# Early raw-key scores for half a token tile, cosines split by parity, joins put first: one core of a Trainium2 chip

## The chip, the cores and the metric

The kernel runs on one core of a Trainium2 chip. The core has a matrix engine (TensorE, PE in the rows; PEld is its load of the stationary operand), a vector engine (VectorE, DVE), an activation engine (ScalarE, ACT), a general engine (GpSimd, POOL) and a sync engine (SyncE, SP), whose queue issues nearly all transfers between device memory and the on-chip memory. Each engine works through its own instructions in the order in which they were written, and waits for others by semaphores. The metric is the time of one execution on the device, in microseconds.

## The reference

Three stages follow each other: attention that keeps the 32 best scores of each row, a gated feed-forward layer, and a second layer with a cosine.

```python
# q, k, v: (4, 8, 576, 64); the result of each stage is (2304, 512)
scores = scale * np.matmul(q, k.transpose(0, 1, 3, 2))
kth = np.partition(scores, -top_k, axis=-1)[..., -top_k:-top_k + 1]   # top_k = 32
scores = np.where(scores >= kth, scores, -1000000000.0)
scores = scores - np.max(scores, axis=-1, keepdims=True)
attn = np.exp(scores); attn = attn / (np.sum(attn, axis=-1, keepdims=True) + 1e-09)
x = np.matmul(attn, v)                       # laid out as (2304, 512)
g = x @ w_gate                               # (512, 1536)
x = (g * (1.0 / (1.0 + np.exp(-g))) * (x @ w_val)) @ w_out
h = x @ w_in                                 # (512, 2048)
out = (h * np.cos(h)) @ w_out2               # (2048, 512)
```

## The kernel before

The 2304 tokens are 18 tiles of 128 rows. A batch has 576 rows, four and a half tiles, so the fifth tile (number 4, rows 512 to 639) holds the last 64 rows of batch 0 and the first 64 of batch 1; tile 13 is cut in the same way. Tiles are grouped into ten chunks: two of one tile, then eight of two.

**Order of work.** The order of every engine's instructions is made when the program is built. Each piece of work is a Python generator that yields steps: an engine, a cost, a function that emits the instructions, and a due time. A planner (class `Plan`) keeps a clock for each engine and always emits, of the steps that are ready by its clock, the one with the smallest due time. What it emits is fixed: on the chip each engine takes its instructions in that order. So a change of a due time, a cost or a wait in the generators moves instructions on all engines.

**Attention.** A unit is one tile of one head: 144 units, `unit_proc`. Its scores are made on PE (lines 590 and 597) in one bank pair `sc`, ACT copies them to a tile `s` (line 602; five such tiles), DVE finds the 32 largest by four MAX8 and three MATCH_REPLACE8 (lines 627 and 630), POOL makes two bounds, ACT masks and exponentiates (lines 658 and 669), PE transposes (line 691) and multiplies with V (lines 744 and 747). In the first three chunks (tiles 0 to 3, all of batch 0) the scores are fp32 matmuls on raw keys `kr` that four early loads bring in. From the fourth chunk on, keys and queries are split into two parts of the rounded format (high part by ACT, line 496, and rest by POOL, line 500), and a score takes two matmuls for each half of the 576 keys. So the 64 rows of batch 0 in tile 4 need split keys of batch 0: eight tiles, two loads each (line 489).

**First feed-forward layer.** `turned_gemm_proc` (line 992) and `gemm_proc` (line 902) multiply x with the gate and value weights into the banks `gv`, and `wout_proc` (line 1066) multiplies the product with the output weights `wo` into the banks `y`. The wo weights are converted once (ACT, and POOL on line 248), stored, and loaded again for each chunk into two buffers (lines 375 and 377), each load after PE is through with the buffer.

**Second layer.** The first product is made with seven products in place of eight (a Strassen scheme): 32 pairs of rows of h, `h_proc`, PE line 1401. Each pair uses three banks. ACT copies partial sums aside (lines 1432 and 1488) and DVE joins them (lines 1445, 1466, 1473, 1479); PE goes on in a bank after the join on 1466 (c22) or the copy on 1479. The weights of the seven products come in four groups, added on DVE (line 1268) and split (ACT line 1284, DVE line 1287). The rows of h are stored to device memory, some with the cosine already applied (lines 1535 to 1552), some raw. Before the change rows whose block f of 128 columns lies in the second or fourth group of four are raw, and take the cosine late, after they are loaded again. The last stage loads h in pieces of four blocks (line 1627), splits them (lines 1643 and 1647) and multiplies (line 1672).

## Time and profile before

| | us |
|---|---|
| median of 3 runs (1238.5 to 1436.85) | 1239.03 |
| the profiled execution | 1239.47 |
| its span, first to last instruction | 1237.7 |

A profile row names an engine, a line of the kernel, an operation, and tiles as out<-in. Busy is the time in which an engine has an instruction at work; a matrix engine that is busy is not always at its best, since matmuls overlap. A wait is put down to the instruction that released it last. The granted clock of the matrix engine is 1.00 at its higher level, 2.4 GHz, and 0.50 at 1.2 GHz.

### The profile page before, as it was taken

To read this page: it belongs to the slowest core of one execution; us is meant where nothing else is said; L and a number is where in the kernel's file an instruction comes from. 1 tells how busy PE (TensorE), PEld (TensorE's weight loads), DVE (VectorE), ACT (ScalarE), POOL (GpSimd) and SP (SyncE) were. 2 spreads that over 40 slices of the span, in tenths; PEclk is the share of its full clock that TensorE was granted. 3 is DMA by queue.
4 is the path that set the end of the run, shared out by engine and by line. 5 is a ranking of instruction groups with operands and counts; after the bars stand their busy time and mean duration, and the time that the engine had idled before them with its cause. 6 is when DMAs were issued, how large, how long until landed. Compare 5 with 4: busy or idle time off the path is not lost.

```text
span 1237.7 us, 23277 instructions
## 1 busy us (share of the span) xinstructions
PE 1179.8 (95%) x7720; PEld 1021.3 (83%) x7720; DVE 1003.4 (81%) x1984; ACT 936.6 (76%) x2085; POOL 575.6 (47%) x1036
## 2 busy tenths in 40 slices
PE   6699988999999999999999999998999999999998
PEld 3477646898888898888898898988899998888887
DVE  6999999999999999998999996267867778544441
ACT  4789988899889889897898887445757668765651
POOL 4898976777677776776777765300000000000000
PEclk9899989999999999999999999999999999999999
DMA  7555555665555565566555533463344376433430
GB/s 256 165 176 163 178 173 186 205 203 178 185 171 170 189 196 154 169 185 187 188 166 174 162 105 95 154 212 117 134 139 135 130 228 212 144 107 115 124 106 26
DMA packets 138984, 199.95 MB, mean 162 GB/s; under 512 B 19312, under 2 KB 88432, under 8 KB 138864
## 3 DMA queue, kind: packets, MB, share of 16 engines
q1 hardware_dynamic: 138704, 198.40, 50.6%
q8 instruction: 61, 1.00, 0.3%
q14 instruction: 59, 0.48, 0.1%
q10 hardware_dynamic: 160, 0.07, 0.0%
HBM read 152.28 MB, written 46.14 MB: 160 GB/s over the span
## 4 chain that ended last, share of the span: by engine, by line
PE 56%; DMA 7%; ACT 7%; DVE 4%; POOL 4%; issue 2%; SPq 0%; POOLq 0%; ACTq 0%; DVEq 0%
PE b L1672 16%; PE b L1401 13%; PE gv L902 10%; PE y L1066 7%; PE av L747 3%; PE sc L597 2%; PE gvl L902 2%; PE tp L691 2%; DMA kx<-in_kT 2%; DVE m L627 1%; DVE w L630 1%; DMA w2d<-w_raw 1%; DMA wo<-wo 1%; DMA qx<-in_qT 1%; DMA w_raw<-in_w 1%
## 5 line engine op out<-in xcount | busy, mean ns | idle before, releaser
L627 DVE MAX8 m<-w 128x8 f32<-128x576 f32 x432 | 310.9, 747 | 1.8
L902 PE MATMUL gv<-x,w 128*128 128x256 f32 x2016 | 284.0, 288 | 2.2 <-ACT hg L869 2.1
L902 PEld LDWEIGHTS gv<-x,w 128*128 128x128 f32 x2016 | 259.2, 190 | 9.3 <-ACT hg L869 3.5
L630 DVE MATCH_REPLACE8 w<-m,w 128x576 f32<-128x576 f32 x288 | 213.2, 742 | 0.0
L1672 PE MATMUL b<-w2o,gp 128*128 128x512 f32 x864 | 202.1, 395 | 0.0
L1672 PEld LDWEIGHTS b<-w2o,gp 128*128 128x128 f32 x864 | 162.1, 188 | 39.0
L1401 PE MATMUL b<-xc,w 128*128 128x288 f32 x1344 | 184.2, 298 | 6.1 <-DVE h L1466 5.6
L1401 PEld LDWEIGHTS b<-xc,w 128*128 128x128 f32 x1344 | 181.5, 189 | 7.6 <-DVE h L1466 6.3
L1066 PE MATMUL y<-wo,gh 128*128 128x512 f32 x400 | 148.7, 414 | 5.2 <-DMA wo<-wo 2.5
L627 DVE MAX8 m<-s 128x8 f32<-128x576 f32 x144 | 107.6, 747 | 17.6 <-ACT s L602 15.9
L658 ACT ACTIVATE e<-s,b 128x576 f32<-128x576 f32 x144 | 114.2, 794 | 9.2 <-POOL b L641 9.0
L669 ACT ACTIVATE e<-e,b 128x576 f32<-128x576 f32 x144 | 114.2, 793 | 2.8 <-POOL b L645 0.2
L602 ACT ACTIVATE s<-sc 128x576 f32<-128x576 f32 x144 | 95.4, 663 | 21.4 <-PE sc L590 15.8
L630 DVE MATCH_REPLACE8 w<-m,s 128x576 f32<-128x576 f32 x144 | 106.8, 742 | 0.0
L691 PE MATMUL tp<-ident,e 128*128 128x128 f32 x648 | 98.9, 276 | 6.4 <-ACT pt L697 3.1
L697 ACT ACTIVATE pt<-tp 128x512 f32<-128x512 f32 (+1 forms) x216 | 101.5, 501 | 4.3 <-PE tp L691 2.9
L1066 PEld LDWEIGHTS y<-wo,gh 128*128 128x128 f32 x400 | 74.7, 188 | 28.0 <-issue 4.1
L597 PE MATMUL sc<-K,q 128*128 128x288 f32 (+1 forms) x512 | 92.2, 307 | 2.6 <-ACT s L602 2.3
L691 PEld LDWEIGHTS tp<-ident,e 128*128 128x128 f32 x648 | 77.9, 142 | 16.9 <-ACT pt L697 6.7
L1066 PE MATMUL y<-wo,gl 128*128 128x512 f32 x208 | 85.6, 418 | 6.1 <-POOL gl L965 3.0
L965 POOL TENSOR_TENSOR gl<-vv,gh 128x256 fp32r<-128x256 f32 x84 | 62.0, 738 | 42.5 <-ACT gh L961 29.0
L597 PEld LDWEIGHTS sc<-K,q 128*128 128x128 f32 (+1 forms) x512 | 73.4, 184 | 8.3 <-ACT s L602 3.7
(115 smaller groups left out, 2093.7 us busy)
## 6 DMA issues: line engine op xcount, KB each, us to landing
wo<-wo SPq DMA_DIRECT2D x96, 512.0 KB, 3.7
gr<-gd SPq DMA_DIRECT2D x72, 256.0 KB, 3.1
w_raw<-in_w SPq DMA_DIRECT2D x32, 511.8 KB, 4.3
V<-in_vP SPq DMA_DIRECT2D x52, 256.0 KB, 3.0
w<-in_w SPq DMA_DIRECT2D x24, 511.5 KB, 5.6
kx<-in_kT SPq DMA_DIRECT2D x64, 144.0 KB, 3.2
wo<-wo SPq DMA_DIRECT2D x36, 256.0 KB, 3.0
gd<-r SPq DMA_DIRECT2D x32, 288.0 KB, 2.2
```

The costliest lines, as they stand in the source:

```text
L597: nc.tensor.matmul(sc[:r1, s, :HALF], q[:, a, (t - t0) * 128:(t - t0) * 128 + r1], k[:, s * HALF:s * HALF + HALF], start=a == 0, stop=a == 1)
L602: nc.scalar.activation(st["s"], sc[:, :, :HALF], AF.Copy)
L627: nc.vector.max(out=st["m"][:, 8 * i:8 * i + 8], in_=st["w"] if i else st["s"])
L630: nc.vector.match_replace(out=st["w"], in_to_replace=st["m"][:, 8 * i:8 * i + 8], in_values=st["w"] if i else st["s"], imm_value=LOWEST)
L658: nc.scalar.activation(st["e"], st["s"], AF.Prelu, bias=st["b"][:, 1:2], scale=SCALE, alpha=STEEP)
L669: nc.scalar.activation(st["e"], st["e"], AF.Exp, bias=st["b"][:, 2:3], scale=1.0, accum_out=smT[c, p, g][:, j:j + 1])
L691: nc.tensor.transpose(st["ps"][:, j - j0], e[:, j * 128:j * 128 + 128], ident)
L697: nc.scalar.activation(pt[:, j0:j1], st["ps"][:, :j1 - j0], AF.Copy)
L902: nc.tensor.matmul(gv[g], W1[f, kk // 2][:, a, g, kk % 2], m, start=kk == 0 and i == 0, stop=kk == KT - 1 and i == 2)
L1066: nc.tensor.matmul(bank, m, w, start=f == 0 and n == 0, stop=f == NF1 - 1 and n == len(terms) - 1)
L1401: nc.tensor.matmul(ps[b], w[:, a, side, kk], x[:, e, kk], start=start and kk == 0 and m == 0, stop=kk == 1 and m == 2, skip_group_check=True)
L1672: nc.tensor.matmul(st["o"], g[:, a, cs], W2O[f][:, b], start=f == 0 and i == 0, stop=f == NF2 - 1 and i == 2)
```

## The change

Eight units' upper 64 rows, those of batch 0 in tile 4, no longer get their scores from split keys. At the start, 64 columns of q for each head (`qe`, with the other head's half of the contraction cleared) are multiplied with the raw keys as fp32, into the banks of the first layer, which are not in use yet; ACT copies the scores to `se`, and four stores bring them to a new tensor `sd` in device memory. The units of tile 4 then compute all 128 rows with batch 1's keys, ACT copies only the lower 64 rows to `s`, and a load on SP's queue brings the upper 64 from `sd`. The first product of the first layer waits until all early scores are copied (`ev_edged`). Split keys of batch 0 are no longer made.

In the second layer, raw rows of h are now those with odd f, not those of the second and fourth group, and the pieces and the order of the last stage's products follow (`members`). The joins and ACT's copies before them are due 90 us before the pair's time, not 30 (all such lines alike, two of them shown). The banks of the pairs rotate over eight from the sixth pair on (`BOTH`), not from the seventh.

```diff
@@ -42,7 +42,7 @@
-BOTH = 6
+BOTH = 5
@@ -56,6 +56,7 @@
+EDGE_DUE = 40.0
@@ -404,7 +405,7 @@
 
     kb_first, kb_last = {}, {}
     for (c, p, h, b), u in kfirst.items():
-        if c < RAWC:
+        if c < RAWC or b == 0:
             continue
         kb_first.setdefault((b, p, h), u)
         kb_last[b, p, h] = max(kb_last.get((b, p, h), 0), klast[c, p, h, b])
@@ -419,8 +420,6 @@
     r_kp = Ring(1)
 
     def k_due(b, p, h):
-        if not b:
-            return due_unit(kb_first[0, 0, 0]) - 60.0 + 2.0 * (2 * p + h)
         return due_unit(kb_first[b, p, h]) - 26.0
 
     def q_due(c, p, g):
@@ -438,7 +437,77 @@
         return i if c < RAWC else RAWC * NP + (i - RAWC * NP) * 2 + h
 
     def k_index(b, p, h):
-        return 1 + NP + kvis[b, p, h]
+        return 2 + 2 * NP + kvis[b, p, h]
+
+    EDGE = S % 128
+    TE = S // 128
+    sd = dram.tile([NP, 128, S], F32, name="sd")
+    r_edge = [Ring(1) for _ in range(2)]
+    ev_edge = [Event() for _ in range(NP)]
+    ev_edged = Event(2 * NP)
+    edge = {}
+
+    def edge_proc():
+
+        def clear():
+            edge["q"] = att.tile([128, NP, 2, EDGE], F32, tag="K", name="qe", bufs=r_k.n)
+            nc.vector.memset(edge["q"], 0.0)
+
+        yield "DVE", 0.5, clear, -1.0, True
+
+        def load():
+            for h in range(2):
+                rows = slice(64 * h, 64 * h + 64)
+                nc.sync.dma_start(edge["q"][rows, :, h],
+                                  qT[:, rows, TE * 128:TE * 128 + EDGE].rearrange("p d n -> d p n"))
+
+        t = yield "DMA", 1.0, load, 2.0, True
+        for p in range(NP):
+            for h in range(2):
+                plan.start(edge_score(p, h), t)
+
+    def edge_score(p, h):
+        n = 2 * p + h
+        due = EDGE_DUE + n
+        yield ev_kr[p]
+        yield r_edge[h].gate(p)
+        ps = gvt if h == 0 else yt
+
+        def qk():
+            for s in range(2):
+                nc.tensor.matmul(ps[s][64 * h:64 * h + EDGE, :HALF], edge["q"][:, p, h],
+                                 KR[p][:, s * HALF:s * HALF + HALF])
+
+        t = yield "PE", 1.25, qk, due, True
+        if n == 2 * NP - 1:
+            r_k.free(1 + NP, t, plan)
+
+        def copy(s):
+            if (p, "s") not in edge:
+                edge[p, "s"] = att.tile([128, S], F32, tag="K", name="se", bufs=r_k.n)
+            rows = slice(64 * h, 64 * h + EDGE)
+            nc.scalar.activation(edge[p, "s"][rows, s * HALF:s * HALF + HALF], ps[s][rows, :HALF], AF.Copy)
+
+        if n and not h:
+            yield ev_edge[p - 1]
+        yield "ACT", 0.33, lambda: copy(0), due, True
+        t = yield "ACT", 0.33, lambda: copy(1), due, False
+        if not h:
+            ev_edge[p].set(t, plan)
+        r_edge[h].free(p, t, plan)
+        if not h:
+            edge[p, "n"] = Event(2)
+            plan.start(edge_store(p, due))
+        edge[p, "n"].set(t, plan)
+        ev_edged.set(t, plan)
+
+    def edge_store(p, due):
+        yield edge[p, "n"]
+        t = yield "DMA", 1.1, lambda: nc.sync.dma_start(sd[p], edge[p, "s"]), due + 2.0, True
+        r_k.free(2 + NP + p, t, plan)
+        ev_sd[p].set(t, plan)
+
+    ev_sd = [Event() for _ in range(NP)]
 
     def k_raw_proc(p):
 
@@ -579,9 +648,11 @@
             yield ev_qr[c, p]
         else:
             for b, r0, r1 in segs:
-                yield ev_k[b, p, h]
+                yield ev_k[b, p, h] if b else ev_sd[p]
             yield ev_q[c, p, g, h]
             q = Q[c, p, g, h]
+        split_row = c >= RAWC and segs[0][0] == 0
+        cuts = [x for x in segs if x[0]]
         yield r_s.gate(u)
 
         def qk():
@@ -591,6 +662,8 @@
                                      KR[p][:, s * HALF:s * HALF + HALF])
                 return
             for b, r0, r1 in segs[::-1]:
+                if not b:
+                    continue
                 k = K[b, p, h]
                 for s in range(2):
                     for a in range(2):
@@ -599,19 +672,25 @@
 
         def copy():
             st["s"] = att.tile([128, 2, HALF], F32, tag="s", name="s", bufs=r_s.n)
-            nc.scalar.activation(st["s"], sc[:, :, :HALF], AF.Copy)
+            if split_row:
+                nc.scalar.activation(st["s"][EDGE:], sc[EDGE:, :, :HALF], AF.Copy)
+                nc.sync.dma_start(st["s"][:EDGE].rearrange("p a b -> p (a b)"), sd[p, 64 * h:64 * h + EDGE])
+            else:
+                nc.scalar.activation(st["s"], sc[:, :, :HALF], AF.Copy)
 
         yield r_sc.gate(u)
-        end = yield "PE", 0.575 * len(segs) if c >= RAWC else 0.98, qk, due - SC_LEAD, True
+        end = yield "PE", 0.575 * len(cuts) if c >= RAWC else 0.98, qk, due - SC_LEAD, True
         if h and (c, t) == (RAWC - 1, SIZES[c] - 1):
             r_k.free(1 + p, end, plan)
         for b, r0, r1 in segs:
-            if c >= RAWC and kb_last[b, p, h] == u:
+            if c >= RAWC and b and kb_last[b, p, h] == u:
                 r_k.free(k_index(b, p, h), end, plan)
         if t == t0 + n - 1 and (h or c >= RAWC):
             r_q.free(q_index(c, p, g, h), end, plan)
         end = yield "ACT", 0.53, copy, due - SC_LEAD + 1.0, True
         r_sc.free(u, end, plan)
+        if split_row:
+            yield "-", 2.5, lambda: None, due, True
         st["s"] = st["s"].rearrange("p a b -> p (a b)")
         yield r_w.gate(u)
         yield r_m.gate(u)
@@ -984,6 +1063,7 @@
             yield ev_gemm[c, 2 * fp - 1]
         yield ev_x[c]
         ring, i = r_gv[fp % 2], GV0[c] + fp // 2
+        yield ev_edged
         yield ring.gate(i)
         bank = gvt[fp % 2].rearrange("p (f g n) -> p f g n", f=2, g=2)
 
@@ -1431,7 +1511,7 @@
                 snaps[name] = pb().tile([128, HN], F32, tag=f"s{name}", name="s", bufs=ring.n)
                 nc.scalar.activation(snaps[name], ps[b], AF.Copy)
 
-            t = yield "ACT", 0.33, fn, due + offset - 30, True
+            t = yield "ACT", 0.33, fn, due + offset - 90, True
             return t
 
         def row(r):
...
@@ -1519,7 +1599,10 @@
     r_s1, r_s2, r_s3 = Ring(2), Ring(1), Ring(1)
     ev_wfree = {(q, n): Event() for q in range(NF2 // 4) for n in range(SEVEN)}
 
-    early = [n for n in range(NCB * NF2) if n % NF2 // 4 not in LATE]
+    def group_of(f):
+        return f // 8 * 2 + f % 2
+
+    early = [n for n in range(NCB * NF2) if group_of(n % NF2) not in LATE]
     turn_of = {n: i for i, n in enumerate(early)}
 
     def cosine(i, h, width, due):
@@ -1611,6 +1694,9 @@
         (t, m) for t in range(AHEAD, NTOK // 128) for m in range(NG)]
     place = {x: n for n, x in enumerate(ORDER)}
 
+    def members(m):
+        return slice(m // 2 * 8 + m % 2, m // 2 * 8 + 8, 2)
+
     def piece_proc(t, m):
         n = place[t, m]
         due = o_due(n) - 6.0
@@ -1625,7 +1711,7 @@
             st["x"] = pools["pb"].tile([128, 2, HN], F32, tag="xr", name="gr", bufs=r_xr.n).rearrange(
                 "p a b -> p (a b)")[:, :DM]
             nc.sync.dma_start(st["x"].rearrange("p (f n) -> p f n", f=4),
-                              gd[:, 4 * m:4 * m + 4, t * 128:t * 128 + 128])
+                              gd[:, members(m), t * 128:t * 128 + 128])
 
         end = yield "DMA", 1.2, load, due - 6.0, True
         ev_gt[n].set(end - 2.0, plan)
@@ -1658,21 +1744,21 @@
         for m in range(NG):
             n = place[t, m]
             yield ev_gp[n]
-            for f in range(4 * m, 4 * m + 4):
+            for v, f in enumerate(range(NF2)[members(m)]):
                 yield ev_w2o[f]
                 if f == 0:
                     yield ring.gate(index)
 
-                def part(f=f, n=n):
+                def part(f=f, n=n, v=v):
                     if f == 0:
                         st["o"] = bank_tile(number)
                     g = GP[n]
-                    cs = slice(f % 4 * 128, f % 4 * 128 + 128)
+                    cs = slice(v * 128, v * 128 + 128)
                     for i, (a, b) in enumerate(((0, 0), (1, 0), (0, 1))):
                         nc.tensor.matmul(st["o"], g[:, a, cs], W2O[f][:, b], start=f == 0 and i == 0,
                                          stop=f == NF2 - 1 and i == 2)
 
-                end = yield "PE", 0.7, part, o_due(n) + f % 4 * 0.7, False
+                end = yield "PE", 0.7, part, o_due(n) + v * 0.7, False
             r_xc.free(SEVEN * NCB + n, end, plan)
         yield r_ot.gate(t)
 
@@ -1687,6 +1773,7 @@
 
     for p in range(NP):
         plan.start(k_raw_proc(p))
+    plan.start(edge_proc())
     for c, p in ev_qr:
         plan.start(q_raw_proc(c, p))
     for i, (_, kind, *which) in enumerate(split):
```

The order on three engines moves as follows. On PE, at the start of the program (`kr` raw keys, `qr` and `qe` queries, `sc` scores, `tp` transposes, `rx` normalising factors); before:

```order
L590 MATMUL sc<-kr,qr 128x288 x14
L691 MATMUL tp<-ident,e 128x128 x9
L794 MATMUL tp<-ident,rx 128x128
L590 MATMUL sc<-kr,qr 128x288 x2
L744 MATMUL av<-pt,vtail_106 128x128
L747 MATMUL av<-pt,V 64x128 x8
L590 MATMUL sc<-kr,qr 128x288 x2
L691 MATMUL tp<-ident,e 128x128 x9
```

and after the change:

```order
L661 MATMUL sc<-kr,qr 128x288 x12
L478 MATMUL gv_100<-kr,qe 64x288
L478 MATMUL gv_101<-kr,qe 64x288
L478 MATMUL y_102<-kr,qe 64x288
L478 MATMUL y_103<-kr,qe 64x288
L661 MATMUL sc<-kr,qr 128x288 x2
L770 MATMUL tp<-ident,e 128x128 x8
L478 MATMUL gv_100<-kr,qe 64x288
L478 MATMUL gv_101<-kr,qe 64x288
L770 MATMUL tp<-ident,e 128x128
L478 MATMUL y_102<-kr,qe 64x288
L478 MATMUL y_103<-kr,qe 64x288
L873 MATMUL tp<-ident,rx 128x128
```

The early scores stand between the sixth and the tenth unit's scores; the rest keeps its place.

On SP's queue, where the fourth chunk's scores begin (`wo` the two weight buffers, `wo_65` their store, `kx` and `qx` keys and queries to be split, `y` results of the first layer); before:

```order
L514 DMA qx<-in_qT 64x2x256 x2
L1111 DMA y_63<-yo 128x2x128
L375 DMA wo<-wo_65 128x512 x3
L1111 DMA y_63<-yo 128x2x128
L489 DMA kx<-in_kT 64x576 x2
L375 DMA wo<-wo_65 128x512 x3
L489 DMA kx<-in_kT 64x576 x2
L541 DMA V<-in_vP 128x512
```

and after:

```order
L558 DMA kx<-in_kT 64x576 x2
L1191 DMA y_63<-yo 128x2x128
L376 DMA wo<-wo_65 128x512 x2
L677 DMA s<-sd 64x576
L1191 DMA y_63<-yo 128x2x128
L376 DMA wo<-wo_65 128x512 x2
L677 DMA s<-sd 64x576
L583 DMA qx<-in_qT 64x2x256 x2
```

The key loads of batch 0 are gone, and the loads of the early scores stand behind weight loads, two before each of the first two.

On DVE, in the second layer, around the third group of weights (`w_14` to `w_20` split weights, `wr` their sums, `h` joins, `r` cosines); before:

```order
L1287 TENSOR_TENSOR w_14_11544<-wr,w_14_11544 128x512
L1287 TENSOR_TENSOR w_15_11555<-wr,w_15_11555 128x512
L1268 TENSOR_TENSOR wr<-wr 128x512
L1287 TENSOR_TENSOR w_19_11566<-wr,w_19_11566 128x512
L1268 TENSOR_TENSOR wr<-wr 128x512
L1287 TENSOR_TENSOR w_16_11589<-wr,w_16_11589 128x512
L1268 TENSOR_TENSOR wr<-wr 128x512
L1287 TENSOR_TENSOR w_17_11603<-wr,w_17_11603 128x512
L1287 TENSOR_TENSOR w_20_11576<-wr,w_20_11576 128x512
L1287 TENSOR_TENSOR w_18_11609<-wr,w_18_11609 128x512
L1466 TENSOR_TENSOR h<-b,s_11521 128x288
L1473 TENSOR_TENSOR h<-b,s 128x288
```

and after, where line 1348 is 1268 of before, 1367 is 1287, 1525 is 1445, 1546 is 1466, 1553 is 1473 and 1559 is 1479:

```order
L1553 TENSOR_TENSOR h<-b,s 128x288
L1367 TENSOR_TENSOR w_14_11518<-wr,w_14_11518 128x512
L1546 TENSOR_TENSOR h<-b,s_11491 128x288
L1367 TENSOR_TENSOR w_15_11530<-wr,w_15_11530 128x512
L1348 TENSOR_TENSOR wr<-wr 128x512
L1525 TENSOR_TENSOR h<-b,s 128x288
L1348 TENSOR_TENSOR wr<-wr 128x512
L1559 COPY h<-b 128x288
L1367 TENSOR_TENSOR w_16_11567<-wr,w_16_11567 128x512
L1367 TENSOR_TENSOR w_17_11579<-wr,w_17_11579 128x512
L1348 TENSOR_TENSOR wr<-wr 128x512
L1367 TENSOR_TENSOR w_19_11533<-wr,w_19_11533 128x512
```

The joins stood behind the seven splits and stand between them now.

## Rows read from the trace of the kernel before

**Rows 1.** Page, part 1: busy time, share of the span, instructions.

```profile
PE 1179.8 (95%) x7720; PEld 1021.3 (83%) x7720; DVE 1003.4 (81%) x1984; ACT 936.6 (76%) x2085; POOL 575.6 (47%) x1036
```

**Rows 2.** Busy time by stretch, us from the span's start.

```profile
core 0: us, PE busy (x) PEld busy (x) DVE busy (x) ACT busy (x) POOL busy (x), PEclk, DMA share, GB/s
...
27.00:64.00 37.00, 23.90 (x146) 16.82 (x145) 35.78 (x79) 29.52 (x64) 31.41 (x60) 0.91 0.54 175
...
128.00:230.00 102.00, 90.36 (x509) 64.38 (x508) 97.25 (x197) 93.14 (x213) 78.22 (x118) 0.97 0.57 179
230.00:757.00 527.00, 517.47 (x3896) 462.49 (x3894) 509.25 (x1050) 457.30 (x1116) 376.48 (x702) 1.00 0.55 173
757.00:850.00 93.00, 91.32 (x644) 83.24 (x644) 46.03 (x93) 44.99 (x107) 19.59 (x34) 1.00 0.51 162
850.00:890.00 40.00, 33.85 (x230) 32.14 (x229) 30.61 (x55) 29.55 (x60) 0.00 (x0) 0.96 0.33 114
890.00:1030.00 140.00, 140.00 (x1052) 140.00 (x1051) 104.04 (x193) 94.36 (x184) 0.00 (x0) 1.00 0.47 161
1030.00:1238.00 208.00, 204.10 (x883) 164.46 (x881) 99.78 (x152) 119.52 (x202) 0.00 (x0) 1.00 0.39 115
```

**Rows 3.** Waits of PE, 128 to 230: total us, times, longest.

```profile
PE y L1066 <- POOL wo L248: 3.2, 3, 2.7
PE y L1066 <- DMA wo<-wo: 2.7, 1, 2.7
PE sc L597 <- ACT s L602: 2.3, 4, 0.8
```

**Rows 4.** The same table by stretch, at three stretches of lower clock.

```profile
157.80:161.20 3.40, 3.40 (x17) 1.72 (x16) 3.37 (x8) 2.61 (x5) 3.32 (x4) 0.50 0.35 98
171.50:174.90 3.40, 3.40 (x12) 2.29 (x11) 3.29 (x9) 2.04 (x5) 2.23 (x4) 0.50 0.52 162
861.00:864.40 3.40, 3.40 (x15) 3.39 (x15) 1.91 (x5) 2.21 (x5) 0.00 (x0) 0.50 0.33 107
```

**Rows 5.** Timeline of PE, early: start, us, what, count [idle before <- releaser].

```profile
30.49 1.14 PE L590 MATMUL sc<-kr,qr 128*128 128x288 f32 x4
...
51.93 0.43 PE L794 MATMUL tp<-ident,rx 128*128 128x128 f32 x1 [4.04 <-POOL rx L783]
...
64.29 1.03 PE L992 MATMUL gv<-w,xw 128*128 128x256 f32 x4
```

**Rows 6.** Chain that ended last, second layer; timeline of PE, tile 4's first score.

```profile
886.63 144.27 PE b L1401 x1080
...
172.19 2.87 PE L597 MATMUL sc<-K,q 128*128 128x288 f32 x8
```

**Rows 7.** Tile kx, 90 to 250: ns min/median/max; POOL's timeline, first and eighth.

```profile
L496 ACT ACTIVATE K<-kx x16: 669/690/747, 99.9 to 241.5; 128x576 fp32r<-128x576 f32 x16
L500 POOL TENSOR_TENSOR K<-kx,K x16: 1399/1410/1699, 101.8 to 243.1; 64x576 fp32r<-64x576 f32 x16
...
DMA to landing us min/median/max: 2.6/2.9/3.8
...
151.69 1.40 POOL L500 TENSOR_TENSOR K<-kx,K 64x576 fp32r<-64x576 f32 x1
```

**Rows 8.** Waits of DVE, 128 to 230.

```profile
DVE m L627 <- ACT s L602: 1.4, 4, 0.6
```

**Rows 9.** Waits of SP's queue, 165 to 250.

```profile
SPq L375 <- PE y L1066: 4.9, 4, 2.1
```

**Rows 10.** Waits of PE, 850 to 890; timelines of DVE and PE there.

```profile
PE b L1401 <- DVE h L1466: 5.6, 3, 3.2
PE b L1401 <- DVE h L1479: 0.6, 1, 0.6
...
858.68 1.89 DVE L1287 TENSOR_TENSOR w<-wr,w 128x512 fp32r<-128x512 f32 x3
860.48 0.45 DVE L1466 TENSOR_TENSOR h<-b,s 128x288 f32<-128x288 f32 x1
...
860.99 3.25 PE L1401 MATMUL b<-xc,w 128*128 128x288 f32 x12 [3.20 <-DVE h L1466]
885.02 1.05 PE L1401 MATMUL b<-xc,w 128*128 128x288 f32 x6 [1.02 <-DVE h L1466]
```

**Rows 11.** Page, part 5 (busy, mean ns | idle before); part 6's view (KB, us to landing).

```profile
L602 ACT ACTIVATE s<-sc 128x576 f32<-128x576 f32 x144 | 95.4, 663 | 21.4 <-PE sc L590 15.8
...
gd<-h SPq DMA_DIRECT2D x32, 288.0 KB, 2.4
```

More of the change, by code (lines that the diff above doesn't have):

```diff
@@ L1444, in c11 @@
             yield r_ha.gate(k)
-            t = yield "DVE", 0.37, lambda: nc.vector.tensor_add(row(0)[:, :HN], ps[1], snaps[0]), due + 3.0 - 30, True
+            t = yield "DVE", 0.37, lambda: nc.vector.tensor_add(row(0)[:, :HN], ps[1], snaps[0]), due + 3.0 - 90, True
             free(1, t)
@@ L1465, in c22 @@
             yield r_hb2.gate(k)
-            t = yield "DVE", 0.37, lambda: nc.vector.tensor_add(row(1)[:, HN:], ps[0], snaps[2]), due + 6.0 - 30, True
+            t = yield "DVE", 0.37, lambda: nc.vector.tensor_add(row(1)[:, HN:], ps[0], snaps[2]), due + 6.0 - 90, True
             r_s3.free(k, t, plan)
@@ L1472, in c12 @@
             yield e_s2
-            t = yield "DVE", 0.37, lambda: nc.vector.tensor_add(row(0)[:, HN:], ps[2], snaps[1]), due + 8.0 - 30, True
+            t = yield "DVE", 0.37, lambda: nc.vector.tensor_add(row(0)[:, HN:], ps[2], snaps[1]), due + 8.0 - 90, True
             free(2, t)
@@ L1478, in c21 @@
         def c21():
-            t = yield "DVE", 0.36, lambda: nc.vector.tensor_copy(row(1)[:, :HN], ps[0]), due + 8.5 - 30, True
+            t = yield "DVE", 0.36, lambda: nc.vector.tensor_copy(row(1)[:, :HN], ps[0]), due + 8.5 - 90, True
             free(0, t)
@@ L1488, in fn @@
                 nc.scalar.activation(snaps[2], ps[2], AF.Copy)
-            t = yield "ACT", 0.33, fn, due + 4.0 - 30, True
+            t = yield "ACT", 0.33, fn, due + 4.0 - 90, True
             e_s3.set(t, plan)
```

## The prediction

> **What bounds the kernel now.** Read the busy shares first, and then do not stop there: TensorE (PE) is busy 95% of the span, VectorE (DVE) 81% and ScalarE (ACT) 76% [rows 1], which says that PE is the engine to shorten, not where. The table by stretch says where [rows 2]. From 27 to 64 us PE is busy 23.9 of 37 and DVE 35.8 of 37: top-k on DVE sets the pace, PE has room. From 128 to 230 us all four engines are near full (PE 90.4, DVE 97.3, ACT 93.1 of 102, POOL 78.2), so PE loses 11.6 us to waits on three others. From 230 to 757 PE is busy 517.5 of 527, and from 757 to 850, with the top-k done, 91.3 of 93: here PE is the bound, and a microsecond that it is ahead at 230 is still there at 850. From 850 to 890 it is idle 6.2 of 40. From 890 to 1030 and from 1030 to 1238 it is busy 140.0 and 204.1: nothing to gain there, only to lose.
>
> Then the waits, stretch by stretch. Between 128 and 230 the large ones are POOL's conversion of an output weight wo (3.2 us, one of 2.7) and the load of such a weight (2.7), then score copies on ACT (2.3) [rows 3]. Twice in this stretch, just after such an idle time, the granted clock is 0.50 for 3.4 us, the lower of its levels (1.2 GHz) [rows 4]; each of these costs some 1.7 us of PE work more. Between 850 and 890 nearly all of the idle time waits for the join on line 1466 [rows 10]: DVE takes a run of weight splits that ends at 860.5 before it, and PE's next matmul starts at 860.99. The clock halves there once too [rows 4].
>
> **The change, part by part.** Sums are against the profiled execution's own 1239.47 us (1237.7 of span and 1.8 around it), 0.4 above the median of 1239.03.
>
> *Early scores.* Sixteen fp32 matmuls of 288 columns are added, with a 64-column stationary operand. Two such matmuls make the four records of 1.14 us in [rows 5], so sixteen take 8 x 1.14 = 9.1 us. In the new order they stand between the sixth and the tenth unit's scores, at about the stretch in which PE has 13.1 us idle in 37 [rows 2], one wait of 4.0 us among it [rows 5]. ACT gets sixteen copies of 288 columns: a 576-column copy is 0.66 us [rows 11], so 0.33 (half) to 0.66 each, 5.3 to 10.6 us, and ACT has 7.5 idle in that stretch [rows 2]. This cover is thin: ACT is full for some 25 us, and the transposes of the first two heads come late by an estimated 3 us. What then waits has slack: PE's next transposes waited 4.0 us for POOL anyway [rows 5]. DVE gains one clearing of 512 columns before its first score has come. Two small loads and four stores of 288 KB join SP's queue; a 288 KB store lands in 2.4 us [rows 11], and the weights behind it are needed no sooner than POOL gets to them. I charge 0.5 us; bounds 0 and 3 (the whole lateness of the first two heads).
>
> *No split keys of batch 0.* Eight tiles go: sixteen load issues, eight ACT copies of 0.69 and eight POOL subtractions of 1.41 us, so 5.5 us of ACT and 11.3 of POOL; the first eight subtractions of the trace, which are these, run from 101.8 to 153.1 us [rows 7]. PE loses 32 matmuls of 288 columns. In the solid train of the second layer's first product 1080 of this width take 144.27 us, 0.134 each [rows 6], so 4.3 us, none of it before 172.2 [rows 6], where PE work begins to count in full: **-4.3**.
>
> *Stalls in 128 to 230.* With POOL and SP lighter, the waits for the converted weight and for its load (2.7 and 2.7) and the two half-clock stretches behind them (1.7 each) can go: 8.8 us at most, 0 at least. DVE limits it: it is idle only 4.75 us of the 102 [rows 2] and gets no less work. I take half, **-4.4**, inside that limit.
>
> *Eight score loads.* Each of the eight units of tile 4 now needs 64 of its rows from device memory before its first MAX8. The load goes through SP's one queue, and in the new order it stands behind weight loads that wait for PE to finish with a buffer. So what is queued behind a waiting weight load is now DVE's own input, and behind DVE the transposes that PE takes in order. No such load exists before. Nearest rows: a key load lands 2.9 us after its issue [rows 7], a weight load on SP waited 4.9 us in four times for PE, 1.2 each [rows 9], and the ACT copy that runs beside it takes 0.66 [rows 11]. One that is fully exposed costs 2.9 + 1.2 - 0.66 = 3.4 us. Hidden ones cost nothing; the lower bound is 0, the upper 8 x 3.4 = 27.5. How much is hidden depends on how far scores run ahead of DVE. Between 128 and 230 DVE waited for a score copy four times, 1.4 us in all [rows 8], so the lead is about zero for a few units and more for the others. In the new order the first two loads are the worst placed (the second stands behind weight buffers that PE frees only after that unit's own matmuls); I take those, part exposed: **+2.5**.
>
> The Trainium skill speaks against this step: its page "DMA: Bandwidth & Descriptors", section "Anatomy of one DMA", puts about 2.0 us of fixed cost on each DMA, and has its semaphore waits served by the issuing sequencer before dispatch. An estimate by that page with nothing hidden is 8 x 2.0 = 16 us in place of 2.5. No row here shows a transfer that lands in much less, so on the price rule and rows are near each other; how much is hidden is a matter of this kernel's order, and the sum goes by the rows.
>
> *Joins first, banks from the sixth pair.* The joins (lines 1445 to 1479) and ACT's copies before them get 60 us more of priority, and in the new DVE order they stand between the weight splits, not behind them. Idle time of 6.2 us is up [rows 10] and one half-clock stretch (1.7): 0 to -7.9. The price is that the splits come later by the joins put between them, 0.45 us each [rows 10]; PE wants them a few pairs later. With the rotation of the eight banks from the sixth pair on, the sixth and seventh no longer share three banks, so the waits of about 1 us in 881 to 887 go with it. I take **-6.0**.
>
> *Cosines by parity.* The same number are early and late. Each pair now has one, where pairs had two or none. In 890 to 1030 DVE is busy 104.0 and ACT 94.4 of 140, and PE never waited [rows 2]. The last pairs before 1030 now have cosines of their own while the first pieces of the last stage are made, with a quarter of DVE still free. Cost 0, by that cover; if it failed, the first pieces would be late by a few us, once.
>
> Sum: 0.5 - 4.3 - 4.4 + 2.5 - 6.0 = -11.7, so 1227.8, and against the median **1227.5 us**. With the middle terms at their nearer bounds the forecast's own range is 1221 to 1234. Chance 0.50.
>
> **Rivals.**
> *Slower: the score loads starve DVE.* Place: the eight units of tile 4, from 172 us on [rows 6]. Price: 3.4 us each, 27.5 for all, in place of 2.5, so 1227.5 + 25 = 1252.5. For: SP's queue is in order, and the lead of scores is near zero here [rows 8]. Against: less ACT and POOL work just before should lengthen that lead. It decides the sign when the loss passes the other terms' 14.2 us, so from five exposed units on. Chance 0.15. The page's fixed cost alone, fully exposed, is this rival's milder form: an estimate of 1241.
>
> *Stalls only move.* In 128 to 230 ACT and DVE stay almost as full, so PE waits as long for others; and at 850 to 890 the later weight splits take back most of the joins' gain. Then 0.5 - 4.3 + 2.5 - 2 = -3.3, so 1235.5. For: four full engines at once. Against: the two largest waits of PE there name exactly the POOL and the load queue that get lighter [rows 3]. Chance 0.20.
>
> *All of it works.* Score loads hidden, 8.8 and 7.9 gone: -4.3 - 8.8 - 7.9 = -21, so 1218. It needs more than the DVE slack of 4.75. Chance 0.12.
>
> The remaining 0.03 is for things not named here, on either side.
>
> **Range and chances.** The range reaches from the last rival to most of the way to the first: 1217 to 1247; above it lies part of the slower rival, below it a little of the best case. A difference of 2% (24.8 us) is about what a measurement of this kernel can tell from no change. Below 1214.3 only an overshoot of the best case lies: 0.03. Above 1263.8 the slower rival would need more than its full price: 0.03. Within: 0.94.
>
> **What would show it.** Early scores: PE's first matmul of line 992's kind (now line 1072) still near 64.3 us [rows 5]. Split keys and stalls: PE idle in 128 to 230 well under 11.6 us, and fewer half-clock stretches there. Score loads: DVE's waits for s by DMA between 165 and 250, some 2.5 us in all; over 14 makes the first rival true. Joins: no wait of PE on the c22 join over 1 us, and none of the half clock, in 840 to 890. Parity: no idle PE from there to the last matmul. The prediction is wrong in its main step if the second layer's first matmul starts no more than 2 us earlier than before, or if the idle 6.2 us come back.

## Result: 1227.9 us, ratio 0.9916

The changed kernel takes 1227.89 us (median of 6 runs, 1223.99 to 1230.96), the kernel before 1238.54 beside it: ratio 0.9916, 95% interval [0.9892, 0.9941], so 10.4 us less by the ratio. Of the six runs of the kernel before, one of 1436.85 us is a slow execution and is not in the ratio. Timed again in another group of runs the changed kernel took 1225.42 beside 1238.14: 0.9897 [0.9883, 0.9912], 12.7 us less. By the bound of 2% that is no change; by the intervals it is faster by 0.6 to 1.2%. The forecast was 1227.5. The profiled execution is one of 1227.0 us, with a span of 1225.1.

The busy shares after, against [rows 1]:

```profile
PE 1174.1 (96%) x7720; PEld 1018.1 (83%) x7720; DVE 1001.4 (82%) x1985; ACT 937.6 (77%) x2093; POOL 564.1 (46%) x1028
```

PE is busy 5.7 us less and POOL 11.5 less; ACT, which lost eight copies and got sixteen smaller ones, as much as before. The table by stretch (columns as in [rows 2]):

```profile
27.00:64.00 37.00, 27.87 (x156) 17.92 (x155) 34.55 (x76) 34.09 (x76) 30.31 (x58) 0.86 0.61 205
...
128.00:230.00 102.00, 90.44 (x521) 65.39 (x520) 95.20 (x195) 92.81 (x211) 72.41 (x115) 0.98 0.59 182
230.00:757.00 527.00, 516.00 (x3908) 464.04 (x3908) 514.66 (x1063) 461.26 (x1123) 380.66 (x708) 1.00 0.56 174
757.00:850.00 93.00, 90.42 (x628) 82.48 (x627) 42.09 (x84) 44.06 (x103) 14.94 (x25) 0.98 0.50 162
850.00:890.00 40.00, 39.80 (x298) 39.34 (x297) 35.65 (x67) 31.37 (x65) 0.00 (x0) 1.00 0.39 132
890.00:1030.00 140.00, 140.00 (x1019) 138.00 (x1018) 105.74 (x195) 98.12 (x188) 0.00 (x0) 1.00 0.51 171
```

Two things are to be seen. In 128 to 230 PE idles as long as before, 11.56 us against 11.64. In 850 to 890 it idles 0.2 us where it idled 6.2. Where the time went is read from two marks of PE's timeline: the first run of 24 matmuls of the second layer's first product, and the first matmul of the last stage. Before:

```profile
847.22 3.37 PE L1401 MATMUL b<-xc,w 128*128 128x288 f32 x24
...
1030.73 1.56 PE L1672 MATMUL b<-w2o,gp 128*128 128x512 f32 x6
```

and after:

```profile
842.87 3.37 PE L1481 MATMUL b<-xc,w 128*128 128x288 f32 x24
...
1018.07 0.87 PE L1758 MATMUL b<-w2o,gp 128*128 128x512 f32 x3
```

The first layer is 4.35 us shorter, the second layer to its last stage 8.3 (183.51 to 175.20). Together 12.7, and the two profiled executions differ by 12.5.

### The profile page after: what moved, and what is told of

The parts are those of the page before. It is cut to its first block, busy times and chain, and to the rows that moved or that the text cites. A ratio compares the mean times of both kernels' runs of the same rounds, so it can differ in the third digit from the quotient of the medians.

```text
span 1225.1 us, 23258 instructions
## 1 busy us (share of the span) xinstructions
PE 1174.1 (96%) x7720; PEld 1018.1 (83%) x7720; DVE 1001.4 (82%) x1985; ACT 937.6 (77%) x2093; POOL 564.1 (46%) x1028
## 4 chain that ended last, share of the span: by engine, by line
PE 66%; DVE 8%; ACT 8%; DMA 8%; POOL 5%; issue 3%; SPq 1%; POOLq 0%; ACTq 0%; DVEq 0%
PE b L1758 16%; PE b L1481 13%; PE gv L981 12%; PE y L1146 9%; DVE m L706 4%; DVE w L709 3%; PE tp L770 3%; PE av L826 3%; DMA wo<-wo 3%; PE sc L670 3%; PE gvl L981 2%; DMA y<-yo 2%; DMA qx<-in_qT 2%; PE gv L1072 1%; ACT e L748 1%
## 5 line engine op out<-in xcount | busy, mean ns | idle before, releaser
L706 DVE MAX8 m<-s 128x8 f32<-128x576 f32 x144 | 107.3, 745 | 15.2 <-ACT s L679 12.9
L679 ACT ACTIVATE s<-sc 128x576 f32<-128x576 f32 x136 | 91.0, 669 | 18.4 <-PE sc L661 15.5
L670 PE MATMUL sc<-K,q 128*128 128x288 f32 x480 | 86.0, 304 | 1.7 <-ACT s L679 1.1
L826 PE MATMUL av<-pt,V 128*64 128x256 f32 (+3 forms) x832 | 75.1, 323 | 0.0
```

The costliest lines, as they stand in the source:

```text
L670: nc.tensor.matmul(sc[:r1, s, :HALF], q[:, a, (t - t0) * 128:(t - t0) * 128 + r1], k[:, s * HALF:s * HALF + HALF], start=a == 0, stop=a == 1)
L706: nc.vector.max(out=st["m"][:, 8 * i:8 * i + 8], in_=st["w"] if i else st["s"])
L826: nc.tensor.matmul(av[64 * h:64 * h + 64, r0:r1], m[:, j, h], pt[:, 5 * h + j, r0:r1], start=False, stop=j == 3)
```

## The experiments

Every kernel was timed in five rounds beside the kernel before, whose median was 1235.78 to 1239.19 us from group to group; the ratio is to the runs of the same group, so ratios compare better than times. The marks are those two in the one profiled execution.

| kernel | us | ratio, 95% interval | first mark | between the marks |
|---|---|---|---|---|
| before | 1238.5 | | 847.22 | 183.51 |
| joins, banks | 1231.37 | 0.9942 [0.992, 0.9964] | 847.48 | 177.57 |
| joins | 1234.14 | 0.9966 [0.9948, 0.9984] | 846.48 | 178.75 |
| parity | 1240.54 | 1.0016 [0.9998, 1.0033] | 846.42 | 183.96 |
| early scores | 1238.58 | 0.9999 [0.9983, 1.0014] | 843.49 | 183.77 |
| all but early scores | 1228.59 | 0.9925 [0.991, 0.9941] | 846.87 | 176.45 |
| whole, first | 1227.89 | 0.9916 [0.9892, 0.9941] | 842.87 | 175.20 |
| whole, again | 1225.42 | 0.9897 [0.9883, 0.9912] | 847.24 | 174.87 |

**The late parts.** First the joins and the banks, in the kernel before:

```diff
-BOTH = 6
+BOTH = 5
-            t = yield "ACT", 0.33, fn, due + offset - 30, True
+            t = yield "ACT", 0.33, fn, due + offset - 90, True
...
```

and the same with - 90 for - 30 on the five other lines of the joins and their copies.

> The kernel before with the joins due 90 us early and the eight-bank rotation from the sixth pair, nothing else. My theory (joins no longer stand behind weight splits): the first layer as before, PE's wait between the second and the eighth pair from 6.2 us to under 1, the half-clock stretch at 861 gone, so 6 to 8.5 us less than the kernel before, about 1231. Rival (stalls only move; the changed kernel's gain there comes from parity, which halves the cosines of the first pairs): 2 us less or nothing, 1236 to 1239.

Measured 0.9942, so 7.2 us less (4.5 to 9.9): the theory, and not the rival. The 6.2 us of waits for joins [rows 10] are gone, but a new one of 1.35 us comes behind them: PE's timeline of this kernel has

```profile
867.06 22.65 PE L1401 MATMUL b<-xc,w 128*128 128x288 f32 x168
891.05 2.14 PE L1401 MATMUL b<-xc,w 128*128 128x288 f32 x14 [1.35 <-DVE h L1466]
```

The join that was put in front of the weight splits now stands behind a step of a cosine: on DVE, line 1543 starts at 889.89 and the join at 890.55. The joins alone, with BOTH at 6:

> The kernel before with the joins due 90 us early alone; banks as before, so the sixth and the seventh pair still share three banks. Theory: the wait of 3.2 us and the half clock at 861 go, the waits of 1.3, 1.0 and 0.6 us at 881 to 887 stay at least in part: 5 to 6 us less, about 1233. Rival (the order on DVE is all of it, banks do nothing): as with the banks, 8 us less.

Measured 4.2 us less (2.0 to 6.4), under the 5 to 6 of the theory but not to be told from them; the 8 of the rival is out. Waits of 1.12, 1.12 and 0.54 us for joins remain in front of matmuls between 878 and 893 in its timeline, where the kernel with both has the one of 1.35. So the banks bring 1.2 us more between the marks, and 2.8 in the medians, whose intervals overlap.

Parity alone, the kernel before with the changed grouping:

```diff
-    early = [n for n in range(NCB * NF2) if n % NF2 // 4 not in LATE]
+    def group_of(f):
+        return f // 8 * 2 + f % 2
+
+    early = [n for n in range(NCB * NF2) if group_of(n % NF2) not in LATE]
...
```

> The kernel before with raw rows by parity of f alone. Theory: cost and gain 0, within 1.5 us of the kernel before, the waits on the join of line 1466 as before. Rival (half the cosines in the first pairs clear DVE for the joins): 3 us less or more, with those waits smaller.

Measured 1.0016 [0.9998, 1.0033]: nothing, or up to 4 us lost. All the old waits for joins are still there.

**The early scores.** The whole change with - 30, BOTH = 6 and the old grouping put back:

> The kernel before with the early raw-key scores alone. Theory: the first layer ends 4 to 6 us earlier (4.3 us of PE work gone, stalls of 128 to 230 smaller, two score loads exposed by 2.1 us in all, 0.5 to 1.3 us lost before 64 us), the second layer waits as before: about 1234. Rival one (the gain of the first layer in the changed kernel was the order's luck): no difference, or slower by 2 or more. Rival two (the eight loads starve DVE): 10 us slower.

Measured 0.9999 over 12 runs: no difference. Its profiled execution, which was the fastest of the twelve, does end the first layer 3.7 us earlier. So either the gain is there in some executions only, or that execution was a lucky one. To tell, and to see whether the parts add up, the three late parts together and the whole again were run on one chip:

> The kernel before with joins first, banks from the sixth pair and cosines by parity, without the early scores. Theory A (the three late parts work together, the early scores add little): the stretch after the seventh pair, which the joins and banks alone lengthened by 2.7 us, comes back to 143 us, so 8.5 us less than before, about 1230.5; the whole change then stands only 0 to 3 us below it. Theory B (parity gives nothing, the early scores bring 4 us on top): the stretch stays at 145 us, 7 us less than before, about 1232, and the whole change stands 4 to 5 us below it.

> The whole change once more, beside the others on one chip. Theory A (sum of its parts measured one by one, with early scores at 0): 1231 to 1232. Theory B (as timed first, with a gain of 4 us in the first layer that the early scores alone did not show): 1228.

Measured 1228.59 and 1225.42, both under what their theories said. The late parts together give 9.3 us by the ratio, where joins and banks gave 7.2 and parity none; with parity no wait for a join is left in 845 to 1220, the 1.35 us above included. That is an interaction, shown by the wait that is gone: with the joins in front parity takes 1.1 us between the marks (one profile each), where alone it took nothing. By the ratios it is 2 (0.9942 to 0.9925), but their intervals overlap, so in the time it is not shown. The early scores add 3.2 us on top in the medians; the intervals of the two ratios touch ([0.991, 0.9941], [0.9883, 0.9912]), and alone they gave none, so I take 0 to 3.

The second profile of the whole change was of a run of 1231.03 us, the slowest of its five and 4.0 above the first one's, and shows how unsteady the gain is. The same program ends the first layer at the old time, and most of the loss is one stretch; the first profile there, and then the second:

```profile
390.00:450.00 60.00, 58.61 (x458) 52.84 (x457) 58.97 (x125) 52.19 (x125) 44.99 (x83) 1.00 0.65 202
```

```profile
390.00:450.00 60.00, 55.63 (x425) 50.47 (x423) 57.02 (x122) 50.47 (x123) 42.85 (x81) 1.00 0.65 199
```

with these waits of PE in the second, where the first has one of 1.1 us for wo and 0.3 for hg:

```profile
PE y L1146 <- DMA wo<-wo: 2.4, 1, 2.4
PE tp L770 <- ACT pt L776: 1.5, 2, 0.9
```

One late weight load and two waits for ACT here take PE 3.0 us (58.61 to 55.63) of the 4.35 that the first layer had won.

**The terms of the early part, one by one.** The 32 matmuls issued after all:

```diff
             for b, r0, r1 in segs if split_row else segs[::-1]:
                 if not b:
-                    continue
+                    b, r1 = 1, 64
```

> The whole change, but the 32 matmuls of 288 columns that it drops are issued after all, with batch 1's keys, and overwritten by the next. By the term of the sum (each matmul 0.134 us on PE, all of it in stretches where PE work counts) the first layer ends 4.3 us later, so 4 us above the whole change of the same call. Rival (PE waits for DVE and ACT there, so its work is hidden): no more than 1 us above it.

Measured 1232.16, ratio 0.9947 [0.9934, 0.996]: 6.7 us above the whole change of the same group, whose interval lies clear below, and 4.3 above its first timing. The term is real and no smaller than expected. The step's cost in the planner was put back with the matmuls, so part of the 6.7 may be another order; how much is not shown. How much an order alone does was asked of the due time:

```diff
-EDGE_DUE = 40.0
+EDGE_DUE = 44.0
```

> The whole change with the early scores due 4 us later, so that the planner makes another order of the same work around them. Theory (the early scores' own work is small, but each new order gains or loses some us by luck in 64 to 230): 1 to 4 us away from the whole change, on either side, with first-layer waits at other places. Rival (the order is robust): within 1 us of it.

Measured 1228.19, 0.9919 [0.9906, 0.9932]: 2.8 above the whole change of the same group, with intervals that overlap by a little, and level with its first timing. That an order alone moves the time by 1 to 4 us is not excluded and not shown; where the early part's own gain is 0 to 3, that is the limit of what these runs tell. Without the eight loads of scores:

```diff
-            if split_row:
-                nc.scalar.activation(st["s"][EDGE:], sc[EDGE:, :, :HALF], AF.Copy)
-                nc.sync.dma_start(st["s"][:EDGE].rearrange("p a b -> p (a b)"), sd[p, 64 * h:64 * h + EDGE])
-            else:
-                nc.scalar.activation(st["s"], sc[:, :, :HALF], AF.Copy)
+            nc.scalar.activation(st["s"], sc[:, :, :HALF], AF.Copy)
```

> The whole change without the eight loads of early scores: ACT copies all 128 rows as before, so 64 rows of tile 4's units hold scores against batch 1's keys; everything else, early scores and their stores too, stays. The two waits of DVE for the load (2.1 us in all) go. Theory A (DVE sets the pace in 128 to 230, so its waits count): 1 to 3 us less than the whole change, 1223 to 1225. Theory B (PE, not DVE, counts, and other waits take over): within 1 us of it.

Measured 0.9914 [0.9891, 0.9936], 1224.28 us: the time is the one of theory A, but the kernel before took 1235.78 in this group, 2.8 less than in the first, and by the ratio this is not to be told from the whole change. DVE's waits for s are gone and its waits for w by ACT rose from 1.9 to 3.2 us. With the loads issued by ACT behind its own copy:

```diff
-                nc.sync.dma_start(st["s"][:EDGE].rearrange("p a b -> p (a b)"), sd[p, 64 * h:64 * h + EDGE])
+                nc.scalar.dma_start(st["s"][:EDGE].rearrange("p a b -> p (a b)"), sd[p, 64 * h:64 * h + EDGE])
```

> The whole change with the eight score loads issued from ACT's own queue, right behind the copy of the other 64 rows, not from SP's. If the 2.1 us of waits come from standing behind weight loads on SP, DVE's first MAX8 of the first two units waits under 1 us in all and the time falls by 0 to 2 us. If they come from the transfer itself (over 3 us against 0.66 for the copy), they stay near 2 us, and so does the time.

Measured 0.9918 [0.9895, 0.994]; 1223.7 us is the lowest median of all, but its own kernel before was at 1235.78, so no version is shown to beat the change. DVE's waits for s fell only from 2.1 to 1.6 us, so the place in SP's queue is not the most of that price. Nor does the transfer alone make it: in the kernel with the early scores due at 44 all eight loads go out on SP, the first at 163.02 and not 168.87, and DVE waits for none of them in 165 to 250. What counts is how long before its need a load goes out.

**The splits kept.** Batch 0's keys are loaded, copied and subtracted again (eight tiles), into their load tile and for nobody. They are kept as plain fp32, and a subtraction takes 1.15 us there, not 1.41, so a little less work comes back than had gone:

```diff
     def k_due(b, p, h):
+        if not b:
+            return due_unit(kfirst[RAWC, 0, 0, 0]) - 60.0 + 2.0 * (2 * p + h)
...
-            K[b, p, h] = att.tile([128, S], F32R, tag="K", name="K", bufs=r_k.n)
+            K[b, p, h] = att.tile([128, S], F32R, tag="K", name="K", bufs=r_k.n) if b else st["x"]
```

> The whole change, but the eight loads, ACT copies and POOL subtractions of batch 0's keys are still done (into their own load tile, and used by nobody), at the priority that they had. The prediction's stalls term says that the lighter POOL, ACT and SP queues bring 4.4 us in 128 to 230: the time rises by about 4, PE idle there from 11.6 to some 16, and the wait for the converted wo is back above 2.5 us. Rival (waits there only change names, so this work was hidden): within 1 us of the whole change.

Measured 1242.78, ratio 1.0062 [1.0039, 1.0084]: 15 to 17 us above the two medians of the whole change (18 to 20 by the ratios), where 4 was the expectation, and slower than before. PE idles 15.5 us in 128 to 230, as expected, and DVE 15.2. The wait for POOL's wo, expected above 2.5, did not come back (none is in PE's list); PE waits 7.3 us for the load of wo instead. The loss is all in the first layer: the first mark is at 859.52, 16.65 later than in the first profile of the change, and 175.93 lie between the marks. It is on DVE's path: of the 576 MAX8 the 97th comes 0.6 us earlier than in the changed kernel (130.39 for 131.03), the 145th 13.9 later (214.75 for 200.81). DVE's waits in 128 to 230:

```profile
DVE m L711 <- DMA s<-sd: 7.3, 3, 3.6
DVE w L299 <- ACT w L295: 3.8, 4, 2.9
DVE m L711 <- ACT s L684: 2.8, 2, 2.5
```

This looks like the rival of the prediction, score loads that starve DVE. So the loads were given to ACT's queue here too, with the same edit as above and nothing else:

> The kernel with the splits kept (1242.8 us, 14.7 above the median of the change as first timed), but with its eight score loads issued from ACT's queue; nothing else moves. Theory A (the 14.7 us are the score loads that stand behind key and weight loads on SP: DVE's waits for them were 8.1 us there, and PE's half clock followed): DVE waits for them under 3 us in all, and the time comes down by 8 to 14 us, to 1229 to 1235. Theory B (the eight copies on ACT and subtractions on POOL themselves fill the stretch): it stays within 3 us of 1242.8.

Measured 1242.85, ratio 1.0061 [1.0037, 1.0085]: the time did not come down. But the waits did not either. DVE's list has 2.3 us for s by DMA, and 4.7 put down to ACT's pt:

```profile
DVE w L299 <- ACT w L295: 4.9, 4, 3.1
DVE m L711 <- ACT pt L781: 4.7, 1, 4.7
DVE m L711 <- DMA s<-sd: 2.3, 2, 1.9
DVE m L711 <- ACT s L684: 2.2, 2, 1.7
```

The wait of 4.7 is one for a score load too: that load goes out at 183.15 and lands 4.2 us later, at 187.37, and the MAX8 starts at 187.46. So DVE waits 7.0 us for these loads here, against 7.3. The under 3 of theory A was not reached, and this run does not say what such waits cost in time. It speaks against the place on SP as what makes the loads late: they go out just behind the start of their unit's first score on either queue (181.74 for 180.50 on SP, 183.15 for 182.01 on ACT). What is late stands ahead of the loads: tile 4's scores themselves. For the first unit ACT's copy of the lower rows begins at 182.14 with the splits kept, and at 170.19 in the changed kernel, 12.0 earlier; MAX8 starts 2.6 us after the copy's start in the one (184.78) and 3.6 in the other (173.75), so the load adds less there, not more. All splits of keys and queries go through one load tile, one after the other. In the changed kernel the first two of batch 1 come at

```profile
117.52 1.41 POOL L569 TENSOR_TENSOR K<-kx,K 64x576 fp32r<-64x576 f32 x1
...
164.60 1.41 POOL L569 TENSOR_TENSOR K<-kx,K 64x576 fp32r<-64x576 f32 x1
```

before the change the first one of batch 1 came at 160.20, behind the eight of batch 0, and in the kernel with the splits kept (loads on SP) it comes at

```profile
170.52 1.41 POOL L573 TENSOR_TENSOR K<-kx,K 64x576 fp32r<-64x576 f32 x1
```

Tile 4's first score starts on PE at 172.19 before [rows 6]. After the change, and with the splits kept:

```profile
166.82 0.80 PE L670 MATMUL sc<-K,q 128*128 128x288 f32 x4 [0.73 <-ACT s L679]
```

```profile
180.50 1.09 PE L675 MATMUL sc<-K,q 128*128 128x288 f32 x4
```

The kept splits also run some 16 us later than they did before: the first is loaded at 94.73, not 76.55, and copied on ACT at 115.61, not 99.94, in an order that has the early scores ahead of them. So the 15 to 20 us are not the price of eight splits at their old place but of splits and early scores together. How they divide was not tried.

## Why the prediction came out right, point by point

The sum was -11.7, and -10.4 and -12.7 were measured. That it came so near is in part luck: two errors offset each other. Up to the first mark the sum has -5.7 (0.5 - 4.3 - 4.4 + 2.5); the first profile has -4.35, the second 0, and the medians give the early part 0 to 3 us. Behind the first mark it has -6.0; the two profiles have -8.3 and -8.6, and the late parts alone brought 9.3 in time. (Against the median of 1239.03 the sum gives 1227.3, not the 1227.5 that was written; it changes nothing.)

**Early scores, +0.5.** Line 1072's first matmul starts at 65.56, not near 64.29 [rows 5], but at 65.40 in the kernel with all parts but the early scores too, so the delay is not shown to be theirs. The cover held: PE is busy 27.87 of the 37 us, and ACT 34.09. Two details were off: a store lands in 5.2 to 6.9 us, not 2.4 [rows 11] (the four go out within some 6 us, and the DMA share is 1.05 in 57 to 64), and the profile puts a wait of PE of 0.8 us down to one.

**32 matmuls, -4.3.** Right, or under-sized: 4.3 and 6.7 above the two timings of the change when they are kept, another order included.

**Stalls in 128 to 230, -4.4.** This step failed as it was put: it counted waits that go, and not what PE waits for next. The waits named in [rows 3] did shrink, those on POOL's wo from 3.2 to 0.8 and those on the load of wo from 2.7 to 2.3, and of two half-clock stretches [rows 4] one is left. But PE's idle time is the same. Its waits there after:

```profile
PE tp L770 <- ACT pt L776: 3.7, 3, 2.2
PE y L1146 <- DMA wo<-wo: 2.3, 4, 1.0
PE y L1185 <- ACT yo L1179: 1.3, 2, 0.6
PE sc L670 <- ACT s L679: 1.1, 2, 0.7
...
PE y L1146 <- POOL wo L249: 0.8, 1, 0.8
```

ACT, which got no less work, took over: PE's waits for it there are 7.3 us in all, 5.2 before. Half of the rival "Stalls only move" is true, the half on this stretch. What the dropped splits did move is another thing, which the prediction had only as a remark against its first rival: tile 4's scores start 5.4 us earlier (166.82 for 172.19). With the splits kept they start 13.7 us later than that, and DVE idles 15.2 us of the 102. What the lead is worth by itself is not shown: the kernel with early scores alone has 4.8 us of it too (167.41) and is no faster than the kernel before.

One premise stays open. The prediction takes PE for the bound from 230 to 850. But in all fourteen profiles the first mark comes 83.5 to 86.4 us after DVE's last MAX8, which moves from 755.56 to 774.20 among them. Here before, after, and with the splits kept:

```profile
763.25 0.76 DVE L627 MAX8 m<-w 128x8 f32<-128x576 f32 x1
...
756.47 0.76 DVE L706 MAX8 m<-w 128x8 f32<-128x576 f32 x1
...
774.20 0.76 DVE L711 MAX8 m<-w 128x8 f32<-128x576 f32 x1
```

So the end of the first layer follows the end of the top-k. DVE is busy 514.66 of the 527 us from 230 to 757 after the change, and PE 516.00; which of the two sets the pace there no run separates.

**Eight score loads, +2.5.** The trace has 2.1 us, in the two loads named, on DVE's timeline:

```profile
173.75 0.76 DVE L706 MAX8 m<-s 128x8 f32<-128x576 f32 x1 [1.19 <-DMA s<-sd]
...
179.49 0.76 DVE L706 MAX8 m<-s 128x8 f32<-128x576 f32 x1 [0.94 <-DMA s<-sd]
```

In the time the price is not more than the runs can show, as the kernel without them tells. Waits of the size that the first rival names came only with the splits kept, where DVE waited 7.3 us for these loads in this stretch; that these waits, and not the late scores, made that kernel slow is not shown. After the change the loads land 3.1, 4.0 and 4.8 us (least, median, most) after issue. The Trainium skill's fixed cost of about 2.0 us ("DMA: Bandwidth & Descriptors", section "Anatomy of one DMA") is under the least of these, and that section gives it for transfers issued by GpSimd, while these go out on SP's queue; the measurement decides. The estimate of 16 us, by that figure with nothing hidden, did not come.

**Joins and banks, -6.0.** The mechanism was right, and so was the size for these two alone: -5.9 between the marks, and 7.2 (4.5 to 9.9) in the time. With parity beside them it is -7.1 to -8.6 between the marks in three profiles, about the upper bound of 7.9. I had kept back 2 us for splits that come late. With joins and banks alone a loss of that size did come, but from a step of a cosine (the 1.35 us at 891), and parity took it away.

**Parity, 0.** Right alone (no gain shown), not in company: with the joins in front it removes a wait of 1.35 us, 1.1 us between the marks.

**The named checks.** No half clock and no wait for a join in 840 to 890, as forecast; PE's train from 862.47 on has no gap in the table. A new half-clock stretch stands at 798, behind a wait of 1.7 us for ACT's yo:

```profile
797.80:801.20 3.40, 3.40 (x15) 3.04 (x14) 2.53 (x5) 3.40 (x9) 0.00 (x0) 0.54 0.13 39
```

and costs some 1.7 us (half of 3.4) of the first layer's lead. The second layer's first matmuls start 4.35 us earlier, so the test that would have made the main step wrong was passed by the first profile; the second, at 847.24, would have failed it.

## What to carry to other kernels

Work that is taken off a chain with one buffer moves what comes next in that chain, so its busy time is not all there is to price: look for the first consumer's start as well. When several engines are full at once, the largest named waits going away says little, for the next engine takes their place; and when a change moves joins ahead, look for what now stands behind them, for the part that seems worth nothing alone may be the one that removes it. A gain of 3 us is less than two profiled executions of one program differed by here (4.0 us), so it is not to be credited to a cause from one profile. And a wait is put down to the instruction that released it last by the profile: where a load lands just before the wait ends, as at 187.37 above, it is the load, whatever the list says.

## Not expected of the hardware

Two fp32 matmuls with 64 stationary columns, one into the lower and one into the upper 64 rows, started side by side in places (PE's timeline of the changed kernel, first four of one head in a row, then of both):

```profile
30.70 1.18 PE L478 MATMUL gv<-kr,qe 128*64 128x288 f32 x4
...
34.42 0.46 PE L478 MATMUL y<-kr,qe 128*64 128x288 f32 x1
34.44 0.46 PE L478 MATMUL gv<-kr,qe 128*64 128x288 f32 x1
34.72 0.41 PE L478 MATMUL y<-kr,qe 128*64 128x288 f32 x1
34.73 0.41 PE L478 MATMUL gv<-kr,qe 128*64 128x288 f32 x1
```

Eight records start within 0.8 us from 34.42 and end at 35.63, so they take 1.21 us, while four of one head in a row take 1.18 us at 30.70; the granted clock is 1.00 in both places. The estimate of 9.1 us for all sixteen matmuls did not count on that.
